# Where the second group's last projections stand, and what the warm-up products read

## The chip, the cores and the metric

The kernel runs on one core of one Trainium2 chip. The metric is the time of one execution on the device in microseconds (us). Engines are named as in the profile: PE does matrix products, PEld loads their weights, DVE, ACT and POOL do elementwise work, SP issues transfers (POOL and ACT issue some too). PE writes its results into PSUM, which DVE and ACT read; everything else lies in SBUF or in device memory.

## What is computed

The input x has 2048 rows of 512 numbers. Two branches are computed from it and mixed row by row.

```python
def A(x, wqkv, wo):                       # attention, 32 heads of 16, window of 256
    q, k, v = split((x @ wqkv))
    scores = einsum("bhqd,bhkd->bhqk", q, k) * 16 ** -0.5
    scores = where((i - j >= 0) & (i - j < 256), scores, -1e9)
    return einsum("bhqk,bhkd->bhqd", softmax(scores), v) @ wo
def B(x, w_gate, w_up, w_down):           # feed-forward, 1792 wide
    return (silu(x @ w_gate) * (x @ w_up)) @ w_down
g = sigmoid((x * gate_w).sum(-1, keepdims=True))
out = g * A(x) + (1 - g) * B(x)
```

## The kernel before

All products are float32 products made of three cheaper ones: each operand is split into a rounded high part and a low rest (`split`, ACT makes the high part, POOL or DVE the rest), and high x high, high x low and low x high are summed in PSUM.

The 2048 rows are cut into four columns `c` of 512, the 32 heads into eight groups `g` of four. `proj(g, c)` makes the queries and keys of one group for one column: twelve products over the whole array into one PSUM tile (L231), then ACT copies that tile out (L274, `ev<-pa` or `ev<-pb`) and splits the copy into `X[g, hf]`, where `hf = c // 2` is the half of the rows. `stack(g, hf)` is a set of twelve transfers on SP's queue, L284 and L285, that lay these parts into the tiles QT and KT from which scores are computed. `X[0, 0]` and `X[1, 1]` lie in the same tiles `xhi`, `xlo` of a pool with one buffer; `X[0, 1]` and `X[1, 0]` (`x01`, `x10`) lie in a pool of their own, `vpool`.

The values V are projected by blocks of 128 rows. The first four blocks are whole-array products. The other twelve go by fours: `vproj2` makes two blocks at once in two lanes, each on 64 of the array's 128 rows (L251, `64*128`), into two tiles named `pb` or two named `pa`. Each name has two buffers in PSUM. When a lane pair is done ACT copies both tiles into `vs` (L442), and after each second block POOL issues a store of `vs` to device memory (`vd<-vs`, L445): eight stores in all. `vs` and V's weights `wvh`, `wvl` lie in `vpool` too.

`stage1(g, b)` computes score products (L301) only for their row maxima, which DVE takes (L303). For group 0 these products stand between V's lane products. `put_max` sends the maxima through device memory into a row of QT (L314 to L319). `stage2(g, b)` computes the scores again (L343, into two buffers named `ps2`), ACT takes their exponentials (L345) into a tile `pt`, and POOL masks them.

The part around the change runs in this order: the projections of both groups for columns 0 and 1 (with V's first blocks between), group 0's columns 2 and 3, V's lane blocks with stage 1 of group 0, then group 1's columns 2 and 3 into `pb`, then `stack(1, 1)` and four loads of V (`load_v`, L330). There `vpool` is closed and `ptp`, the pool of the `pt` tiles, takes its memory. The main loop follows: for each step it runs one product of stage 1 of the next group, one of stage 2 of this group, and three lane pairs of another projection or of the feed-forward's gate and up products (L251), first into two `pa` tiles, then into two `pb` tiles; every fourth step it adds the products of the exponentials with V (L367). All engines execute their own queue in the order in which the code was written (`manual_schedule`).

At the very start nine 128x128 products (L206) run on a tile of ones, so that PE is busy before the first data arrive. The tile is a part of `KT[0][0]`, which POOL fills with ones by a memset at L203, and which is later filled again by `fill_rows` (L424).

Of the kernel before, what the change touches and what calls it, by code (L numbers as in the profile page):

```python
# [8 lines left out]
F32 = mybir.dt.float32  # L9
# [6 lines left out]
P = 128  # L16
# [4 lines left out]
NCH = S // CH  # L21
# [14 lines left out]
def gated_mix(ctx, tc, xT, xn, w1a, w1b, wqk, wv, wo, wgu, wd, gw, outT):  # L36
# [4 lines left out]
    nc = tc.nc  # L41
# [49 lines left out]
    def run(gen, n=None):  # L91

        while n is None or n > 0:
            if next(gen, run) is run:
                break
            n = n and n - 1
# [5 lines left out]
    def slot(name, dtype=F32R):  # L102
        return stk.tile([P, S], dtype, name=name)

    def halves_of(t):
        n = t.shape[-1] // 2
        return [t[:, :n], t[:, n:]]

    QT = [[slot(f"q0{pr}") for pr in range(2)]]
    KT = [[slot(f"k0{pr}") for pr in range(2)]]  # L110
# [4 lines left out]
    def products(key, c):  # L115
        wh, wl = WT[key]
        return [(wt[:, k], xt[c][:, k]) for k in range(NK) for wt, xt in ((wh, xhi), (wh, xlo), (wl, xhi))]

    def swapped(todo):

        return [todo[n] for k in range(0, len(todo), 3) for n in (k, k + 2, k + 1)]
# [71 lines left out]
    pp = ctx.enter_context(tc.tile_pool(name="pp", bufs=2, space=PSUM))  # L193
# [4 lines left out]
    with ExitStack() as A:  # L198
        sm = A.enter_context(tc.tile_pool(name="sm", bufs=2))


        ones = KT[0][0][:, :P].bitcast(F32)
        nc.gpsimd.memset(ones, 1.0)  # L203
        warm = pp.tile([P, CH], F32, name="pa")
        for _ in range(9):
            nc.tensor.matmul(warm[:, :P], ones, ones, start=True, stop=True)  # L206
# [8 lines left out]
        def kept():  # L215
            return sm.tile([P, CH], F32, name="ev", bufs=EV)
# [3 lines left out]
        def x_pair(pool=None, name="x"):  # L220
            return tuple((pool or sm).tile([P, 2 * CH], F32R, name=f"{name}{w}", bufs=1) for w in ("hi", "lo"))

        def split_qk(g, hf, cc, raw):
            hi, lo = (t[:, cc * CH:(cc + 1) * CH] for t in X[g, hf])
            split(hi, lo, raw, *act)

        def whole(pool, name, todo, done):

            ps = pool.tile([P, CH], F32, name=name)
            for n, (w, x) in enumerate(todo):  # L230
                nc.tensor.matmul(ps, w, x, start=n == 0, stop=n == len(todo) - 1)  # L231
                if n < len(todo) - 1:
                    yield
            done(ps)
            yield
# [30 lines left out]
        def proj(g, c, pool, name):  # L266

            hf, cc = divmod(c, 2)
            if cc == 0:
                X[g, hf] = x_pair() if g == hf else x_pair(vpool, f"x{g}{hf}")  # L270

            def done(ps):
                raw = kept()
                nc.scalar.copy(raw, ps)  # L274
                split_qk(g, hf, cc, raw)
            todo = products(("p", g), c)
            return whole(pool, name, swapped(todo) if g == c == 0 else todo, done)

        def stack(g, hf):
            for pr in range(2):  # L280
                q, k = (halves_of(t[g % 2][pr])[hf] for t in (QT, KT))
                hi, lo = (x[32 * pr:] for x in X[g, hf])
                for b, (qx, kx) in enumerate(((hi, hi), (hi, lo), (lo, hi))):
                    nc.sync.dma_start(q[b::4].bitcast(F32), qx[:32].bitcast(F32))  # L284
                    nc.sync.dma_start(k[b::4].bitcast(F32), kx[64:96].bitcast(F32))  # L285
# [24 lines left out]
        def put_max(g, hf):  # L310

            mt = sm.tile([P, 32], F32R, name="mt", bufs=1)
            mtt = sm.tile([P, 32], F32, name="mtt", bufs=1)
            nc.vector.tensor_scalar(mt, MX[g, hf].rearrange("p h b -> p (h b)"), -1.0, None, op0=ALU.mult)  # L314
            nc.vector.transpose(mtt, mt.bitcast(F32))
            md = dram.tile([4, NB // 2, 4, 32], F32, name=f"md{g}{hf}")
            nc.sync.dma_start(md.rearrange("h b p q -> p (h b) q"), mtt)
            for pr in range(2):
                nc.sync.dma_start(halves_of(QT[g % 2][pr])[hf][63::64].bitcast(F32),  # L319
                                  md[2 * pr:2 * pr + 2].rearrange("h b p q -> h (b p q)"))  # L320
# [188 lines left out]
            run(proj(0, c, pp, "pa"))  # L509
        stack(0, 1)  # L510
        stack(1, 0)


        first = chain(*(stage1(0, b) for b in range(NB)))
# [12 lines left out]
                put_max(0, 0)  # L527
        run(first)
        put_max(0, 1)
        for c in range(2, NCH):  # L530
            run(proj(1, c, pp, "pb"))
        stack(1, 1)
        for n in range(4):
            load_v(n)
        vp.close()
# [161 lines left out]
        for t in range(G * NB + 1):  # L697
# [6 lines left out]
            for hd in range(4):  # L704
# [10 lines left out]
                if hd == 1 and part == 0:  # L715
                    if t:
                        ag, c = divmod(d - 1, NCH)
# [393 lines left out]
```

## Time and profile before

| | |
|---|---|
| median of three executions | 801.77 us (801.17 to 802.30) |
| the profiled execution's own time | 801.55 us |
| its span, first to last instruction | 799.9 us |
| granted PE clock, mean over the span | 1.000 |
| PE busy | 794.2 us (99%) |
| DVE busy | 626.2 us (78%) |
| ACT busy | 432.6 us (54%) |
| POOL busy | 342.1 us (43%) |
| PE's share of the chain that ended last | 98% |

All times in the views are counted from the start of the span; 1.65 us of the profiled execution lie outside it. A timeline row reads: start, length, engine, line, operation, tiles written and read, shapes, how many; in brackets how long the engine sat idle before it and what released it. A product's length overlaps that of the next one, so the pace of PE is read from start to start: 0.23 us for a 512-wide product, or for a pair of lane products.

### The profile page before, as it was taken

The numbers are of one execution on the slowest core, as the hardware profiler recorded it, in microseconds if no ns is written. First come the engines' busy times: TensorE is split into PE (matmuls) and PEld (weight loads), VectorE is DVE, ScalarE is ACT, GpSimd is POOL, SyncE is SP. The second block draws the span as 40 slices with busy tenths as digits, with TensorE's granted clock in tenths as the row PEclk, the third lists the DMA queues.
The fourth block names the chain that finished last, engine by engine and source line by source line (L and its number), as shares of the span: only waits on it lengthen the run. The fifth ranks groups of instructions, "written<-read, shape, count | busy, mean of one in ns | idle before, by whom it ended". The sixth has DMA issues, their size and how long they took to land.

```text
span 799.9 us, 21441 instructions
## 1 busy us (share of the span) xinstructions
PE 794.2 (99%) x8247; PEld 698.2 (87%) x8247; DVE 626.2 (78%) x1689; ACT 432.6 (54%) x883; POOL 342.1 (43%) x643
## 2 busy tenths in 40 slices
PE   9999999999999999999999999999999999999998
PEld 8888999889889989899998998888988888888886
DVE  5397787878886887878776888888675478899896
ACT  7422556565565567555666656555643235554642
POOL 6712456565546556544656454546740111000112
PEclk9999999999999999999999999999999999999999
DMA  8574515425242453351533516425537898717435
GB/s 302 168 217 147 142 69 137 131 90 151 68 153 81 114 168 103 112 156 59 145 111 120 152 51 195 144 90 186 190 105 251 285 342 293 288 57 272 93 55 104
DMA packets 62107, 121.88 MB, mean 152 GB/s; under 512 B 10868, under 2 KB 19828, under 8 KB 61748
## 3 DMA queue, kind: packets, MB, share of 16 engines
q1 hardware_dynamic: 54756, 99.01, 40.1%
q0 software_dynamic: 7104, 21.24, 9.0%
q8 instruction: 65, 1.06, 0.6%
q14 instruction: 38, 0.31, 0.1%
q10 hardware_dynamic: 144, 0.26, 0.1%
HBM read 55.97 MB, written 39.34 MB: 119 GB/s over the span
## 4 chain that ended last, share of the span: by engine, by line
PE 98%; DVE 2%; issue 0%; POOL 0%; POOLq 0%
PE pa L251 24%; PE pb L251 24%; PE ps L301 7%; PE ps L343 5%; PE ps L367 5%; PE ps L87 4%; PE ps L86 4%; PE ps L85 4%; PE pb L367 4%; PE pa L231 2%; PE pb L231 2%; PE pa L87 2%; PE pb L86 2%; PE pa L86 2%; PE pb L87 2%; PE pb L85 2%
## 5 line engine op out<-in xcount | busy, mean ns | idle before, releaser
L303 DVE CUSTOM_DVE_ANT_0 ps<-ps,mask 128x384 f32<-128x384 f32 (+2 forms) x512 | 268.5, 540 | 99.4 <-PE ps L343 52.1
L345 ACT ACTIVATE pt<-ps 128x384 f32<-128x384 f32 (+2 forms) x512 | 238.0, 474 | 127.5 <-PE ps L343 68.0
L347 POOL TENSOR_SCALAR_AFFINE_SELECT pt<-pt 128x256 f32<-128x256 f32 x256 | 110.7, 433 | 197.4 <-ACT pt L345 195.5
L343 PE MATMUL ps<-q,k 64*128 64x384 f32 (+2 forms) x512 | 162.3, 335 | 0.0
L301 PE MATMUL ps<-k,q 63*128 63x384 f32 (+2 forms) x512 | 159.6, 332 | 0.5 <-DVE mx L303 0.5
L251 PE MATMUL pb<-xhi,wh 64*128 64x512 f32 x512 | 117.0, 396 | 0.0
L251 PE MATMUL pb<-xlo,wh 64*128 64x512 f32 x512 | 115.7, 391 | 0.0
L251 PE MATMUL pa<-xhi,wh 64*128 64x512 f32 x512 | 115.7, 394 | 0.0
L251 PE MATMUL pb<-xhi,wl 64*128 64x512 f32 x512 | 115.6, 391 | 0.0
L251 PE MATMUL pa<-xlo,wh 64*128 64x512 f32 x512 | 114.4, 392 | 0.0
L251 PE MATMUL pa<-xhi,wl 64*128 64x512 f32 x512 | 114.3, 391 | 0.0
L301 PEld LDWEIGHTS ps<-k,q 63*128 63x128 f32 x512 | 88.9, 185 | 13.4 <-DVE mx L303 3.3
L350 POOL TENSOR_SCALAR_AFFINE_SELECT pt<-pt 128x256 f32<-128x256 f32 x224 | 98.4, 439 | 0.0
L343 PEld LDWEIGHTS ps<-q,k 64*128 64x128 f32 x512 | 91.3, 185 | 5.2 <-issue 0.2
L303 DVE DVE_READ_ACCUMULATOR2_ANT mx<- 128x1 f32 x512 | 71.4, 139 | 0.0
L367 PE MATMUL ps<-pt,vg 64*32 64x320 f32 (+4 forms) x1408 | 70.6, 344 | 0.0
L367 PE MATMUL pb<-pt,vg 64*32 64x256 f32 (+3 forms) x1360 | 69.9, 349 | 0.0
L251 PEld LDWEIGHTS pb<-xhi,wh 64*128 64x128 f32 x512 | 63.1, 186 | 4.1 <-DVE o L384 0.3
L251 PEld LDWEIGHTS pb<-xhi,wl 64*128 64x128 f32 x512 | 62.6, 185 | 3.6
L251 PEld LDWEIGHTS pa<-xhi,wl 64*128 64x128 f32 x512 | 61.3, 185 | 3.9
L251 PEld LDWEIGHTS pb<-xlo,wh 64*128 64x128 f32 x512 | 62.6, 186 | 0.2
L251 PEld LDWEIGHTS pa<-xhi,wh 64*128 64x128 f32 x512 | 60.8, 186 | 1.9
(303 smaller groups left out, 1601.0 us busy)
## 6 DMA issues: line engine op xcount, KB each, us to landing
kept_h<-ev SPq DMA_DIRECT2D x52, 256.0 KB
od<-o POOLq DMA_DIRECT2D x32, 256.0 KB, 3.5
raw<-wgu SPq DMA_DIRECT2D x28, 256.0 KB
q<-xhi SPq DMA_DIRECT2D x56, 128.0 KB
k<-xhi SPq DMA_DIRECT2D x56, 128.0 KB
outT<-sg POOLq DMA_DIRECT2D x28, 256.0 KB, 4.0
vd<-vs POOLq DMA_DIRECT2D x8, 672.0 KB, 4.9
vg<-vd SPq DMA_DIRECT2D x32, 168.0 KB
```

The costliest lines, as they stand in the source:

```text
L85: nc.tensor.matmul(ps, lh, rh, start=start and i == 0, stop=False, skip_group_check=skip)
L86: nc.tensor.matmul(ps, lh, rl, start=False, stop=False, skip_group_check=skip)
L87: nc.tensor.matmul(ps, ll, rh, start=False, stop=stop and i == n - 1, skip_group_check=skip)
L231: nc.tensor.matmul(ps, w, x, start=n == 0, stop=n == len(todo) - 1)
L251: mm = nc.tensor.matmul(ps[me], w[r], x[r], start=not second and i == 0, stop=bool(second) and i == n - 1)
L301: nc.tensor.matmul(ps[:, :n], QT[g % 2][pr][r, q0:q0 + P], KT[g % 2][pr][r, k0:k0 + n], start=True, stop=True)
L303: mx = nc.vector.tensor_tensor_reduce(out=ps[:, :n], in0=ps[:, :n], in1=mask[:, 3 * P - n:], scale=1.0, scalar=NEG, op0=ALU.add, op1=ALU.m ...
L343: nc.tensor.matmul(ps[:, :n], KT[g % 2][pr][r, k0:k0 + P], QT[g % 2][pr][r, k0:k0 + n], start=True, stop=True)
L345: BEHIND.append(nc.scalar.activation(pt[:, j, :n], ps[:, :n], AF.Exp, scale=SCALE))
L347: nc.gpsimd.affine_select(out=pt[:, :, :P], in_=pt[:, :, :P], pattern=[[0, 2], [1, P]], compare_op=ALU.is_ge, fill=0.0, base=0, channel_mu ...
L350: nc.gpsimd.affine_select(out=pt[:, :, 2 * P:], in_=pt[:, :, 2 * P:], pattern=[[0, 2], [-1, P]], compare_op=ALU.is_ge, fill=0.0, base=-1, ...
L367: nc.tensor.matmul(AV[g, c][h][32 * j:32 * j + 32, q0 - c * CH:q1 - c * CH], VG[4 * g + kb // 4][o, kb % 4, 17 * j:17 * j + 32], PT[g, kb, ...
```

## The change

Two edits. The warm-up products read an array of ones that the program holds as a constant from its start (one column of 128 numbers, read again and again), in place of the tile that POOL fills; the memset goes. And the 24 products of `proj(1, 2)` and `proj(1, 3)`, with `stack(1, 1)`, move from behind V's lane blocks to ahead of them, behind `stack(1, 0)`.

```diff
-        ones = KT[0][0][:, :P].bitcast(F32)
-        nc.gpsimd.memset(ones, 1.0)
+        ones = nc.const_aps.tensor(1.0, [P, P], F32)
         warm = pp.tile([P, CH], F32, name="pa")
         for _ in range(9):
             nc.tensor.matmul(warm[:, :P], ones, ones, start=True, stop=True)
...
             run(proj(0, c, pp, "pa"))
         stack(0, 1)
         stack(1, 0)
+        for c in range(2, NCH):
+            run(proj(1, c, pp, "pb"))
+        stack(1, 1)
 
 
         first = chain(*(stage1(0, b) for b in range(NB)))
...
         run(first)
         put_max(0, 1)
-        for c in range(2, NCH):
-            run(proj(1, c, pp, "pb"))
-        stack(1, 1)
         for n in range(4):
             load_v(n)
         vp.close()
```

Lines behind the removed memset have a number lower by one in the changed kernel. The order of the instructions shows two places.

ACT, where V's last copies end and the main loop begins. Before (`vs<-pa` are the copies of V's last two blocks, `ev<-pb` and `xhi<-ev` belong to the two projections, `pt<-ps` is the first exponential; names in brackets are the semaphores that an instruction waits for, `DMASW0` to `DMASW7` those of V's eight stores in their order, `DMAHW` those of SP's transfers):

```order
L442 COPY vs_129<-pa 128x8x4x16 [waits DMASW5_49,PE_49,Activation_49]
L442 COPY vs_129<-pa 128x8x4x16 [waits Activation_49]
L274 COPY ev<-pb 128x512 [waits PE_49]
L67 CAST xhi<-ev 128x512 [waits DMAHW3_49,DMAHW2_49,DMAHW4_49,DMAHW1_49,DMAHW6_49,DMAHW0_49,DMAHW7_49,Activation_49,Pool_49]
L274 COPY ev<-pb 128x512 [waits PE_49]
L67 CAST xhi<-ev 128x512 [waits Activation_49]
L345 ACTIVATE pt<-ps_1048 128x384 [waits DMAHW2_49,DMAHW3_49,DMAHW1_49,DMAHW4_49,DMAHW0_49,DMAHW5_49,DMASW7_49,DMAHW6_49,DMASW6_49,DMAHW7_49,PE_49,Pool_49]
```

Now:

```order
L441 COPY vs_128<-pa 128x8x4x16 [waits DMASW5_49,PE_49,Activation_49]
L441 COPY vs_128<-pa 128x8x4x16 [waits Activation_49]
L344 ACTIVATE pt<-ps_1047 128x384 [waits DMAHW2_49,DMAHW1_49,DMAHW3_49,DMAHW0_49,DMAHW4_49,DMASW7_49,DMAHW5_49,DMASW6_49,DMAHW6_49,PE_49,DMAHW7_49,Activation_49,Pool_49]
L67 CAST wh<-raw 128x512 [waits DMAHW1_49]
L344 ACTIVATE pt<-ps_1065 128x384 [waits PE_49]
```

The two copies and casts of the projections stand 13 rows earlier, and the first exponential follows V's last copy directly. In both orders it names the last of V's stores, `DMASW7`.

PE, where whole-array products end and V's lane products begin. Before:

```order
L231 MATMUL pa<-xlo_73,wh 128x512 [waits DVE_49]
L231 MATMUL pa<-xhi_72,wl 128x512
L251 MATMUL pb<-wvh,xhi_68 128x512 [waits PE_49] x2
L251 MATMUL pb<-wvl,xhi_68 128x512 x2
L251 MATMUL pb<-wvh,xlo_69 128x512 x2
```

Now:

```order
L230 MATMUL pb<-xlo_73,wh 128x512
L230 MATMUL pb<-xhi_72,wl 128x512
L250 MATMUL pb<-wvh,xhi_68 128x512 [waits Activation_49] x2
L250 MATMUL pb<-wvl,xhi_68 128x512 x2
L250 MATMUL pb<-wvh,xlo_69 128x512 x2
```

The products ahead of the lanes were group 0's last projection into `pa`; they are now group 1's last projection into `pb`, the name that the lanes write next, and the first lane pair names ACT.

## The prediction

> **What bounds the kernel now.** I read the page first (busy shares, then the chain that ended last), and then the timeline engine by engine between 33 and 85 us, where the moved work lies.
>
> ```profile
> PE 794.2 (99%) x8247; PEld 698.2 (87%) x8247; DVE 626.2 (78%) x1689; ACT 432.6 (54%) x883; POOL 342.1 (43%) x643
> PE 98%; DVE 2%; issue 0%; POOL 0%; POOLq 0%
> ```
>
> PE is the bound: 99% busy, and 98% of the chain that ended last. So any time in which PE stands still in the middle is added to the end, and moving PE's work about can win only what PE loses today. The place of the change, on PE's timeline:
>
> ```profile
> 33.15 0.39 PE L231 MATMUL pa<-xhi,wl 128*128 128x512 f32 x1
> 33.47 0.50 PE L251 MATMUL pb<-wvh,xhi 64*128 64x512 f32 x2
> ...
> 71.82 0.39 PE L251 MATMUL pa<-wvh,xlo 64*128 64x512 f32 x2
> 72.05 0.34 PE L301 MATMUL ps<-k,q 63*128 63x384 f32 x2
> 72.31 0.50 PE L231 MATMUL pb<-xhi,wh 128*128 128x512 f32 x1
> ...
> 77.68 0.39 PE L231 MATMUL pb<-xhi,wl 128*128 128x512 f32 x1
> 78.00 0.32 PE L301 MATMUL ps<-k,q 63*128 63x128 f32 x1
> 78.00 0.44 PE L343 MATMUL ps<-q,k 64*128 64x384 f32 x1
> ...
> 79.79 0.44 PE L343 MATMUL ps<-q,k 64*128 64x384 f32 x1
> ```
>
> The reader should see that nothing waits here. V's lanes end at 72.05 with the last two products of stage 1; the 24 projection products run from 72.31 to 77.68; the main loop starts at 78.00, and its third stage 2 product stands at 79.79. The only loss is at switches between whole-array and lane products: 0.26 + 5.37 + 0.32 = 5.95 us from 72.05 to 78.00, where 24 products and the one stage 1 pair ahead of them would take 5.44 + 0.17 = 5.61 at the pace of the whole-array products elsewhere:
>
> ```profile
> 22.66 10.88 PE pa L231 x48
> ```
>
> This row of the chain of waits gives 10.88 / 48 = 0.2267 for one 512-wide product, so 5.44 for 24, and 0.17 for a 384-wide one.
>
> What runs meanwhile on the other engines:
>
> ```profile
> 72.30 1.08 ACT L442 COPY vs<-pa 128x512 f32<-128x512 f32 x2 [2.23 <-issue]
> 78.11 0.59 ACT L274 COPY ev<-pb 128x512 f32<-128x512 f32 x1 [1.44 <-PE pb L231]
> 78.73 0.62 ACT L67 CAST xhi<-ev 128x512 fp32r<-128x512 f32 x1
> 79.25 0.48 ACT L345 ACTIVATE pt<-ps 128x384 f32<-128x384 f32 x1
> ```
>
> ```profile
> DMA to landing us min/median/max: 4.7/4.7/4.7
> ```
>
> ```profile
> 73.67 0.89 POOL L445 DMA_DIRECT2D vd<-vs  x1 [2.42 <-ACT vs L442]
> ```
>
> The landing row is that of this last store alone. V's last copies end at 73.38, POOL issues the store at 73.67, and it lands 4.7 us later, at 78.37. The first exponential writes into memory that the closed `vpool` held, and it names that store among its waits. Today it starts at 79.25 behind ACT's cast, 0.88 us after the landing, so the wait costs nothing. The projections are what hides it: they fill 72.3 to 78.0.
>
> **Edit 1, the warm-up.** It removes one memset from POOL and a wait of PE.
>
> ```profile
> 0.81 0.14 POOL L61 MEMSET edge<- 128x56 f32 x1 [0.29 <-POOLq L1103]
> 0.88 0.20 POOL L203 MEMSET k<- 128x128 f32 x1
> 1.09 0.91 DVE L424 MEMSET q<- 128x1024 f32 x1 [1.09 <-PEq L1103]
> 1.14 4.21 PE L206 MATMUL pa<-k 128*128 128x128 f32 x18 [1.14 <-POOL k L203]
> ```
>
> ```profile
> 4.06 0.62 ACT L67 CAST xhi<-q 128x512 fp32r<-128x512 f32 x1
> 5.00 0.77 PE L231 MATMUL pa<-xhi,wh 128*128 128x512 f32 x1
> ```
>
> PE starts at 1.14, 0.06 after the memset's end (0.88 + 0.20). Without it PE starts as soon as it is released: between 0.81, when POOL does, and 1.09, when DVE starts with an instruction that waits for no data. Behind the warm-up the first real product could go from 5.00 to 4.74 at the earliest, since its cast ends at 4.68. So the gain is 0.05 to 0.26 us. I take 0.15, between the two engines' starts, and none as the lower end, because no product in the trace reads one column again and again; were each of the 18 records a tenth slower, 0.4 us would be lost instead (an estimate). POOL's later memsets no longer wait for PE, which is worth nothing: POOL's next work then waits for ACT.
>
> **Edit 2, ahead of the lanes.** The same 24 products, copies, casts and 12 transfers are issued, so no work is added; only waits change. On PE the last projection starts its last product at 33.15 + 24 x 0.2267 = 38.59. The first lane pair needs both `pb` buffers, and one of them is the projection just finished. Its copy starts 0.43 after the start of the last product (78.11 - 77.68) and takes 0.59: the buffer is free at 39.61 and PE goes on at 39.67, with the 0.06 of the warm-up's wait. Without this it would start at 38.59 + 0.32 = 38.91. **Cost 0.76**, or 0.2 less since the first lane may run one product ahead: I take 0.66. So V's lanes and stage 1 run 5.44 + 0.66 = 6.1 us later than now. On ACT this copy stands behind the cast of the projection before it, which overwrites `xhi` and must wait until `stack(0, 0)` has been read out:
>
> ```profile
> 33.70 0.60 SPq L285 DMA_DIRECT2D k<-xhi  x1
> ```
>
> ```profile
> 37.17 0.22 PE L301 MATMUL ps<-k,q 63*128 63x128 f32 x2
> ```
>
> The last of those transfers is issued at 33.70, and the product at 37.17, which reads what they bring, runs on PE's pace; so they have landed by then, the cast is over by 37.9, and the copy, due at 39.02, is not held. On SP the twelve transfers of `stack(1, 1)` now stand ahead of `put_max(0, 0)`; behind the 57.9 at which `stack(1, 0)` is issued today they take 12 x 0.64 = 7.7 us at the pace of 33.70, to 65.6, and the maxima come at about 63.5 + 6.1 = 69.6: covered, by 4 us. V's loads move forward.
>
> **Edit 2, behind the lanes.** Now the main loop follows the lanes directly. First the PSUM buffers: the loop's first stage 2 product needs a `ps2` buffer that DVE still reads, and its first lane pair needs both `pa` buffers.
>
> ```profile
> 72.42 0.57 DVE L303 CUSTOM_DVE_ANT_0 ps<-ps,mask 128x384 f32<-128x384 f32 x1
> 72.90 0.60 DVE L303 CUSTOM_DVE_ANT_0 ps<-ps,mask 128x384 f32<-128x384 f32 x1
> ```
>
> In times of the run before, to which 6.1 is added, the `ps2` buffers come free at 72.99 and 73.50, the `pa` buffers when ACT's copies end, the second at 73.38. So PE, which could start the loop at 72.22, does its first two steps by about 74.9. The third stage 2 product needs the first `ps2` buffer back, that is the first exponential; and that one waits for the store: it starts at 78.37 + 0.06, takes 0.48, and PE goes on at 78.97. **PE stands still from 74.9 to 78.97, 4.1 us.** Behind the waiting exponential ACT holds the next weight's cast and all further exponentials, and behind these POOL's masks and PE's whole queue.
>
> **The sum.** The third stage 2 product, today at 79.79, comes at 78.97 + 6.1 = 85.07: +5.28. As a check by pieces: +0.66 for `pb`; the loop's first two steps last 78.97 - 72.22 = 6.75 instead of 79.79 - 78.00 = 1.79, +4.96; and what went from 72.05 to 78.00 takes 5.44 ahead of the lanes plus 0.17 instead of 5.95, -0.34: together +5.28. With the warm-up's -0.15: +5.1. PE is the bound from there to the end, so the delay stays. On the profiled execution's own 801.55 (span 799.9 and 1.65 around it) that is 806.7; this execution stands 0.2 below the median of 801.77, so I forecast **806.9**.
>
> **The rivals.** First, *the clock falls in the gap*, and it costs more.
>
> ```profile
> 795.58 0.28 PE L87 MATMUL pa<-hh,xlo 128*128 128x256 f32 x1
> ```
>
> ```profile
> 798.80:799.00 0.20, 0.00 (x0) 0.00 (x0) 0.00 (x0) 0.00 (x0) 0.00 (x0) 1.00 0.00 0
> 799.20:799.40 0.20, 0.00 (x0) 0.00 (x0) 0.00 (x0) 0.00 (x0) 0.00 (x0) 0.50 0.00 0
> ```
>
> ```profile
> 6.43 0.63 PE L231 MATMUL pa<-xhi,wh 128*128 128x512 f32 x1
> 6.86 0.58 PE L231 MATMUL pa<-xlo,wh 128*128 128x512 f32 x1
> ...
> 7.51 0.40 PE L231 MATMUL pa<-xhi,wh 128*128 128x512 f32 x1
> 7.74 0.39 PE L231 MATMUL pa<-xhi,wl 128*128 128x512 f32 x1
> ```
>
> PE's last product ends at 795.86, and some 3.3 us later the granted clock is 0.50. The new gap is longer than that. At the start products stand 0.43 apart, and 0.23 from 7.5 on, after 6 us of work. If the clock falls before PE is back, work runs at half pace for 3.3 us (if the rise takes as long as this fall) to 6.1 (as at the start, 1.14 to 7.27): 1.7 to 3.0 us more, 808.6 to 809.9. Against it: the trace shows a single fall, only 0.8 us shorter than the gap, and nothing says that every gap of this length brings one; chance 0.25. The Trainium skill (TensorE: Matmul & The Clock Gate, part 1) says that activity is judged in free-running windows of about 3.4 us; by that rule a gap of 4.1 holds a whole window in about (4.1 - 3.4) / 3.4 = 2 of 10 executions, an estimate. The 3.3 us at the end of this trace agree.
>
> Second, *the first exponential is not really held until the store lands*: the list of names shows a wait, the trace only that it is over. Then the buffers alone cost: +0.66, the loop's first two steps 74.9 - 72.22 = 2.7 instead of 1.79, -0.34 and -0.15 give +1.1, 802.9. Against it: nothing else would be late today either, so the trace cannot refute it. Chance 0.06.
>
> Third, on the other side, *not slower*: PE keeps its pace at the seam because the store and both buffers come free in time, and only the two saved switches and the warm-up count: -0.34 - 0.15, 801.3. Then the third stage 2 product would stand 1.79 behind the loop's start, at 74.01, its exponential would start by 73.47, and the store would have to land with V's last copy, against 5.0 us later today (78.37 - 73.38). Chance 0.04.
>
> Fourth, *the cast into `xhi` waits longer*: if `stack(0, 0)` is read out later than 38.4, every us beyond that delays the copy and the lanes by a us; 807.9 for one. The row at 37.17 speaks against it. Chance 0.05.
>
> The forecast itself has 0.60; its bounds are 4.5 to 5.7 us (a landing in 4.4 to 4.9, the least and the median of the eight stores, the lane's 0.2 and the warm-up's 0.05 to 0.26), 806.3 to 807.5.
>
> ```profile
> DMA to landing us min/median/max: 4.4/4.9/6.7
> ```
>
> The most, 6.7, is of stores in the midst of `stack`'s transfers, of which none runs beside the last one. The range takes in most of the clock's case: **805.4 to 809.7**. 0.2% of the time, 1.6 us, is about what a measurement tells from no change; the cases two and three and a little beside lie within it or below: faster 0.02, same 0.08, slower 0.90.
>
> **What would show it.** Right: a row of ACT's first exponential waiting some 4 to 5 us for the transfer `vd<-vs`, PE idle for about 4 us near 81 to 85, a hole of 0.6 to 0.8 at 39 before the first lane pair, stage 1's first product near 42.2, the first record on PE near 1.0. Wrong: an exponential within 1 us of V's last copy, or PE busy through 85. A granted clock of 0.50 after the gap would be the first rival. The forecast fails as a whole if the memory of `pt` does not wait for the store.

## The result and the profile after

The changed kernel takes 809.84 us (median; 809.77 to 810.0) against 801.92 for the kernel before (801.17 to 802.3): a ratio of 1.0103, 95% interval 1.0091 to 1.0115. It is slower, as forecast, but by 8 us and not by 5: the time lies 0.14 us above the range's upper end of 809.7, where rival 1 (808.6 to 809.9, chance 0.25) had put it. The profiled execution took 809.83, with a mean granted clock of 0.996 where the one before had 1.000.

The page of the kernel after, busy shares and the chain that ended last:

```profile
span 808.1 us, 21435 instructions
PE 797.8 (99%) x8247; PEld 703.9 (87%) x8247; DVE 625.9 (77%) x1689; ACT 432.6 (54%) x883; POOL 341.5 (42%) x642
PE 87%; DVE 2%; issue 1%; ACT 0%; ACTq 0%
```

PE is the bound still, with the same number of products. It was busy 3.6 us longer and the span is 8.2 longer, so some of the loss is standing still and some is work that went slower. Both are at one place. First the end of V's lanes on ACT and POOL (timelines of the kernel after; line numbers are lower by one than before):

```profile
78.16 1.08 ACT L441 COPY vs<-pa 128x512 f32<-128x512 f32 x2 [2.22 <-issue]
84.70 0.49 ACT L344 ACTIVATE pt<-ps 128x384 f32<-128x384 f32 x1 [5.47 <-DMA md<-mtt]
```

```profile
79.53 0.89 POOL L444 DMA_DIRECT2D vd<-vs  x1 [2.41 <-ACT vs L441]
```

```profile
DMA to landing us min/median/max: 4.9/4.9/4.9
```

V's last copies end at 79.24, the store is issued at 79.53 and lands at 84.43 (the last row is of this store alone), and the first exponential starts at 84.70. The profile puts its 5.47 us of waiting down to `md<-mtt`, a transfer of the maxima; an experiment below shows that it is the store. PE at the same place:

```profile
80.74 0.22 PE L300 MATMUL ps<-k,q 63*128 63x128 f32 x1
85.25 0.69 PE L342 MATMUL ps<-q,k 64*128 64x384 f32 x1 [4.18 <-ACT pt L344]
...
85.84 0.94 PE L250 MATMUL pa<-xlo,wh 64*128 64x512 f32 x2
86.27 0.94 PE L250 MATMUL pa<-xhi,wl 64*128 64x512 f32 x2
...
91.52 0.56 PE L250 MATMUL pb<-xhi,wh 64*128 64x512 f32 x2
91.75 0.56 PE L250 MATMUL pb<-xlo,wh 64*128 64x512 f32 x2
```

PE stands still for 4.18 us; the row at 85.25 is the main loop's third stage 2 product, which stood at 79.79 before: +5.46. Then pairs of lane products follow each other 0.43 us apart, and from 91.4 on 0.23. The same stretch by windows (columns: window, length, busy time of PE, PEld, DVE, ACT and POOL with their counts, granted PE clock, DMA share, GB/s):

```profile
84.50:84.60 0.10, 0.00 (x0) 0.00 (x0) 0.00 (x0) 0.00 (x0) 0.00 (x0) 0.80 0.00 0
84.57:87.97 3.40, 2.72 (x14) 2.72 (x16) 0.36 (x2) 2.26 (x5) 2.02 (x4) 0.50 0.34 103
87.98:91.38 3.40, 3.40 (x20) 3.40 (x19) 0.98 (x4) 0.98 (x2) 0.96 (x3) 0.50 0.61 180
91.30:91.40 0.10, 0.10 (x4) 0.10 (x2) 0.00 (x0) 0.00 (x0) 0.10 (x1) 0.56 0.00 0
```

The clock falls to 0.50 at 84.56 (0.80 in the first row is 0.06 us at 1.00 and 0.04 at 0.50), 0.69 us ahead of PE's return, and rises at 91.39. The end of the span:

```profile
803.86 0.28 PE L87 MATMUL pa<-hh,xlo 128*128 128x256 f32 x1
```

This last product stood at 795.58: +8.28, which is the whole difference between the two profiled executions (809.83 - 801.55). Of it 5.46 is lost by the third stage 2 product, 2.68 from there to 92.4, each product set against the same one of before, and 0.14 in all the rest.

### The profile page after: what moved, and what is told of

It reads as the page before. It is cut to its first block, busy times and chain, and to the rows that moved or that the text cites. A ratio compares the mean times of both kernels' runs of the same rounds, so it can differ in the third digit from the quotient of the medians.

```text
span 808.1 us, 21435 instructions
## 1 busy us (share of the span) xinstructions
PE 797.8 (99%) x8247; PEld 703.9 (87%) x8247; DVE 625.9 (77%) x1689; ACT 432.6 (54%) x883; POOL 341.5 (42%) x642
## 4 chain that ended last, share of the span: by engine, by line
PE 87%; DVE 2%; issue 1%; ACT 0%; ACTq 0%
PE pa L250 22%; PE pb L250 22%; PE ps L300 6%; PE ps L342 5%; PE ps L366 5%; PE ps L86 4%; PE ps L85 4%; PE ps L87 4%; PE pb L366 4%; PE pb L86 2%; PE pb L85 2%; PE pa L86 2%; PE pa L85 2%; PE pb L87 2%; PE pa L87 2%; PE pa L775 1%
## 5 line engine op out<-in xcount | busy, mean ns | idle before, releaser
L300 PE MATMUL ps<-k,q 63*128 63x384 f32 (+2 forms) x512 | 167.2, 332 | 0.5 <-DVE mx L302 0.5
L250 PE MATMUL pa<-xhi,wh 64*128 64x512 f32 x512 | 117.4, 396 | 0.0
L300 PEld LDWEIGHTS ps<-k,q 63*128 63x128 f32 x512 | 94.9, 186 | 12.5 <-DVE mx L302 3.1
```

The source lines that it names most:

```text
L250: mm = nc.tensor.matmul(ps[me], w[r], x[r], start=not second and i == 0, stop=bool(second) and i == n - 1)
L300: nc.tensor.matmul(ps[:, :n], QT[g % 2][pr][r, q0:q0 + P], KT[g % 2][pr][r, k0:k0 + n], start=True, stop=True)
```

## The experiments

Time of the kernel before beside the first four runs: 801.58 us; beside the next four 801.78; beside the last two 802.03.

### Each edit alone

```diff
-        ones = KT[0][0][:, :P].bitcast(F32)
-        nc.gpsimd.memset(ones, 1.0)
+        ones = nc.const_aps.tensor(1.0, [P, P], F32)
```

> The first edit alone, on the kernel before: the warm-up products read the program's constant, the projections stay behind the lanes. Theory: PE starts 0.29 us earlier (0.85 instead of 1.14), and as PE is the bound this is all that changes: 801.6 us, no hole, granted clock 1.00 up to PE's last product. Rival (what the changed kernel gained at its start came from the clock rising earlier in that execution, not from the edit): 801.9.

801.80 us (801.04 to 802.55), ratio 1.0002 (0.9993 to 1.0011): nothing that can be measured. PE's timeline of this kernel shows why:

```profile
0.85 4.02 PE L205 MATMUL pa<-const-float32-1.0 128*128 128x128 f32 x18 [0.85 <-PEq L1102]
4.68 0.50 PE L230 MATMUL pa<-xhi,wh 128*128 128x512 f32 x1
...
6.87 0.49 PE L230 MATMUL pa<-xhi,wh 128*128 128x512 f32 x1 [0.27 <-ACT wh L67]
```

PE starts 0.29 earlier than before and its first real product 0.32 earlier. But some products later it waits for ACT's casts, and these come when the data come. The third stage 2 product of this execution stands 0.16 later than before: the head start is used up by a wait for data.

```diff
         stack(1, 0)
+        for c in range(2, NCH):
+            run(proj(1, c, pp, "pb"))
+        stack(1, 1)
...
         put_max(0, 1)
-        for c in range(2, NCH):
-            run(proj(1, c, pp, "pb"))
-        stack(1, 1)
```

> The second edit alone: the projections and stack(1,1) ahead of the lanes, the warm-up as before. Theory: the whole loss is here: PE idle for 4.2 us near 81 to 85.5 behind the first exponential, clock 0.50 behind it for some 6.8 us, 810.1 us. Rival (the two edits work together, an earlier start shifts where the idle time falls in the clock's judging, so that without it the clock does not fall): 807.3.

809.02 us (808.02 to 809.3), ratio 1.0089 (1.0075 to 1.0103). Edit 2 alone brings 7.4 us of slowdown, both edits together 7.9. Three of the four executions have a mean clock of 0.995 or 0.996, as all four of the changed kernel have; the one of 808.02 has 0.998, half as long at half clock. The rival without a fall (807.3) was in none. PE's timeline and windows of the profiled execution:

```profile
81.08 0.22 PE L301 MATMUL ps<-k,q 63*128 63x128 f32 x1
85.25 0.69 PE L343 MATMUL ps<-q,k 64*128 64x384 f32 x1 [3.85 <-ACT pt L345]
```

```profile
80.05:83.45 3.40, 1.35 (x14) 0.94 (x10) 0.99 (x7) 0.00 (x0) 0.71 (x1) 1.00 0.67 213
83.47:86.86 3.39, 1.61 (x8) 1.61 (x10) 0.00 (x0) 1.77 (x4) 1.07 (x1) 0.50 0.10 18
86.88:90.28 3.40, 3.40 (x21) 3.40 (x20) 0.85 (x4) 0.98 (x2) 1.67 (x5) 0.50 0.88 263
```

Here the fall comes at 83.46, only 2.2 us after PE's last product, and PE had worked for 1.35 of the 3.40 us before it. So the fall isn't the answer to 3.4 us of standing still. The 810.1 that was expected is 0.8 above the profiled execution and 1.1 above the median. The third stage 2 product stands at 85.25 as in the changed kernel, but the stretch at half clock, 83.46 to 90.29, began 1.1 us sooner, while PE stood still, so 2.2 us are lost behind that product and not 2.7.

### What the exponential waits for

The last two V blocks get tiles of their own in `xhi` and `xlo` and one store each, so that none of the memory that `pt` takes over is still being read by the last store; the seventh store's remains.

```diff
+            if b >= NB - 2:
+                t = LASTV[b % 2]
+                nc.scalar.copy(..., ps.rearrange("p (g j e) -> p g j e", j=4, e=DH))
+                nc.gpsimd.dma_start(vd[:, :, b].rearrange("g p e -> p g e"), t)
+                return
             t = vs[b // 2 % 2]
```

> The changed kernel, but the last two blocks of V are copied into the tiles xhi and xlo (idle there) and stored from them by two transfers of 336 KB, so that the memory which the exponentials take over holds only what the seventh store and those before it read. Theory (the first exponential waits for the landing of the last store out of that memory): it starts behind the seventh store's landing, some 3.7 us earlier, at about 81; PE's hole shrinks to about 0.5 us, the clock stays at 1.00, total 803.3. Rival (the profile names the small transfer md<-mtt as what the exponential waited for; it still lands near 84.6): the exponential at 84.7, 809.8.

803.44 us (803.03 to 804.67), ratio 1.0022 (1.0013 to 1.0031). On ACT and on PE of this kernel:

```profile
81.16 0.49 ACT L344 ACTIVATE pt<-ps 128x384 f32<-128x384 f32 x1 [1.59 <-DMA vd<-vs]
```

```profile
81.70 0.44 PE L342 MATMUL ps<-q,k 64*128 64x384 f32 x1 [0.31 <-ACT pt L344]
```

The exponential no longer stands behind the last store but behind the one before it, 3.5 us earlier, the clock stays at 1.00, and 6.4 us are back. The transfers of the maxima were left as they were; SP issues them here at these times:

```profile
80.51 0.57 SPq L316 DMA_DIRECT2D md<-mtt  x1
85.90 0.98 SPq L318 DMA_DIRECT2D q<-md  x2
```

The exponential starts 0.08 us after `md<-mtt` has been issued, and 4.7 us before the transfers that read what it brings are. So the releaser that the profile named was not the cause.

### The hole before the first lane pair

To this kernel the exchange of the two names was added, so that the first lane pair writes `pa`, which was free.

```diff
-            (a0, a1), (b0, b1) = vproj2(b, pp, "pb"), vproj2(b + 2, pp, "pa")
+            (a0, a1), (b0, b1) = vproj2(b, pp, "pa"), vproj2(b + 2, pp, "pb")
```

> The kernel with the last two V blocks stored from other tiles, and besides the two lane names of V exchanged, so that the first lane pair writes pa, which group 0's projections left long ago, and the last one pb. Theory: the hole of 0.74 us at 39 goes, everything behind it comes that much earlier, the seventh store too: 803.44 - 0.74 = 802.7, with the third stage 2 product near 81.0. Rival (the first lane pair waits for something else, or the seam behind the lanes takes up what was won): 803.2 to 803.6.

802.91 us (802.57 to 803.73), ratio 1.0015 (1.0006 to 1.0024). At the place of the hole, in the changed kernel and then in this one:

```profile
38.62 0.50 PE L250 MATMUL pb<-wvh,xhi 64*128 64x512 f32 x1
39.36 0.49 PE L250 MATMUL pb<-wvh,xhi 64*128 64x512 f32 x1 [0.25 <-ACT ev L273]
```

```profile
38.22 0.39 PE L230 MATMUL pb<-xhi,wl 128*128 128x512 f32 x1
38.54 0.50 PE L250 MATMUL pa<-wvh,xhi 64*128 64x512 f32 x2
```

In the changed kernel the second lane starts 0.74 after the first; here both start together, 0.32 behind the last whole-array product. The third stage 2 product comes at 80.59, 1.11 earlier than without the exchange, of which 0.4 us were there at 33 us already. That leaves 0.7 for the hole, as expected. The medians differ by 0.53 only. Most of what stays above the kernel before, 0.80 of 1.1 us, stands there already at 80.59, where the exponential waits for the seventh store. None of the kernels measured here beats the one before. The two switches that a better order would save are worth 0.34 us by the prediction's estimate, and the interval of these measurements is some 0.7 us to each side.

### Half of the move

```diff
         stack(1, 0)
+        run(proj(1, 2, pp, "pb"))
...
         put_max(0, 1)
-        run(proj(1, 2, pp, "pb"))
         run(proj(1, 3, pp, "pb"))
         stack(1, 1)
```

> Only proj(1, 2) runs ahead of V's lanes; proj(1, 3) and stack(1, 1) stay behind them. Theory (the stall is the last store's landing less the work that stands in front of the main loop): the lanes come 2.72 us (12 products) + 0.66 later, the store lands at 73.38 + 3.4 + 0.3 + 4.9 = 82.0, the first exponential starts at 82.2, the third stage 2 product at 82.75, some 2.9 later than before: 804.4 to 804.6, PE idle for about 1.9 us ahead of it and no fall of the clock, as no window of 3.4 us is mostly idle. Rival (the stall is there whenever the loop's first exponential follows on a store at all, whatever lies between): 4 us of idle again, 807 to 810.

806.02 us (805.65 to 806.85), ratio 1.0057 (1.0043 to 1.0071): 1.5 us more than the theory. PE's timeline and windows:

```profile
80.66 0.22 PE L300 MATMUL ps<-k,q 63*128 63x128 f32 x1
82.56 0.44 PE L342 MATMUL ps<-q,k 64*128 64x384 f32 x1 [1.67 <-ACT pt L344]
```

```profile
80.27:83.66 3.39, 1.72 (x17) 1.36 (x15) 0.56 (x4) 1.65 (x4) 1.84 (x2) 1.00 0.22 64
83.68:87.08 3.40, 3.40 (x21) 3.30 (x20) 0.99 (x5) 1.08 (x3) 2.13 (x5) 0.50 0.68 168
```

The stall went as expected: 12 products left in place shorten it from 4.18 to 1.67 us, and the third stage 2 product is at 82.56 where 82.75 was expected. The clock did not: it fell after a standstill of 1.67 us, in a window in which PE was busy for 1.72 of 3.39 us, and stayed down for one window. All four executions have a mean clock of 0.997 or 0.998. The expectation that so short a hole brings no fall was wrong.

### Products that nobody reads, in the hole

The changed kernel with n products into `pb` tiles ahead of the third stage 2 product (the first kernel: 16 into one tile; the others: half of n into each of two):

```diff
+                if t == 0 and hd == 2:
+                    for _ in range(2):
+                        idle = pp.tile([P, CH], F32, name="pb")
+                        for _ in range(n // 2):
+                            nc.tensor.matmul(idle, xhi[0][:, 0, :P], xhi[0][:, 1], start=True, stop=True)
                 if t < g7:
                     run(s2, 1)
```

> The changed kernel with 16 products added whose result nobody reads, 512 columns each, on PE just ahead of the third stage 2 product, so 3.6 us of work in the 4.2 us in which PE stood idle. Theory (8.3 us = 5.5 from the hole and the wait for pb, 2.8 from half pace behind it): idle at most 0.6 us at a time, granted clock 1.00 throughout, the third stage 2 product still at 85.2, total 807.0. Rival (the time behind the hole is lost to a backlog of ACT, POOL and transfers, the clock only goes along): 809.8 or more.

> The changed kernel with 12 full products in the hole, six into each of two pb tiles: PE is idle for 4.2 - 12 x 0.25 = 1.2 us. Theory 1 (the clock falls after a window of the fixed grid of 3.41 us in which PE works for less than some 45%): the worst window is still some 60% busy, no fall in any execution, 806.9 to 807.9. Theory 2 (any hole of more than about 1 us at this place brings the fall, as the one of 1.67 us did in every execution): 808.5 or more.

> The changed kernel with 8 products that nothing reads, four into each of two pb tiles, at the place where PE stands still (two tiles so that the later use of the two pb buffers stays as it was). PE is then idle for 4.2 - 8 x 0.25 = 2.2 us. Theory 1 (the clock falls after a window of 3.41 us that is wholly idle): no fall in any execution, 806.9 to 807.1. Theory 2 (a window that is mostly idle is enough; in the run of edit 2 alone the window that ended with the fall had 1.25 of 3.41 us busy, and the window that ended 69% busy in the run with 16 products brought none): idle of 2.2 us in a window leaves 36 to 40% of it busy, so the clock falls in some executions, half of them at the most, and these take 808.5 to 809.8.

> As before with 4 such products, two into each tile: PE is idle for 4.2 - 4 x 0.25 = 3.2 us, still less than a window of 3.41. Theory 1 (wholly idle window): no fall in any execution, 806.9 to 807.1. Theory 2 (a mostly idle window is enough, limit near 40% busy): it falls in two thirds or more of the executions, median 808.5 to 809.8.

| products | PE idle after them, us | time, us | executions with a fall |
|---|---|---|---|
| 16 | 0 | 807.91 (807.37 to 808.05) | 0 of 4 |
| 12 | 1.12 | 807.59 (807.47 to 807.84) | 0 of 5 |
| 8 | 1.87 | 808.95 (807.27 to 809.77) | 3 of 5 |
| 4 | 2.93 | 808.55 (807.61 to 809.9) | 2 of 4 |
| none (the changed kernel) | 4.18 | 809.84 (809.77 to 810.0) | 4 of 4 |

A fall is counted where the mean clock is 0.998 or less; the others have 0.999 or 1.0. With 16 products PE has more to do and the kernel is 1.9 us faster: the rows of that kernel show the third stage 2 product at the same place, but at full pace.

```profile
81.21 3.92 PE L708 MATMUL pb<-xhi 128*128 128x512 f32 x16
85.17 0.44 PE L342 MATMUL ps<-q,k 64*128 64x384 f32 x1
```

Windows of the kernels with 4, 8 and 12 products, each on the grid of that execution's clock steps; the clock fell at the end of the first two, and not at the end of the third:

```profile
80.63:84.02 3.39, 1.45 (x8) 0.67 (x4) 0.36 (x2) 0.00 (x0) 0.00 (x0) 1.00 0.67 210
```

```profile
82.11:85.50 3.39, 1.52 (x10) 0.97 (x10) 0.00 (x0) 0.91 (x3) 0.00 (x0) 1.00 0.40 122
```

```profile
82.68:86.08 3.40, 2.28 (x15) 1.69 (x16) 0.00 (x0) 1.71 (x4) 0.63 (x1) 1.00 0.13 33
```

Holes of 1.87 and 2.93 us, shorter than a window, brought a fall in some executions and not in others, so a wholly idle window isn't needed. That is the theory of mostly idle windows. (The 1.25 us that the expectation for 8 products names for the window of edit 2 alone is 1.35 in its row.) Its shares were rough: with 8 products half of the executions at the most were expected to fall, and 3 of 5 did; with 4 two thirds or more, and 2 of 4 did, so that the median of 808.55 stands for neither the two that fell (809.23 and 809.9) nor the two that didn't (807.61 and 807.88).

The kernels with 12 and 16 products come out 0.9 to 1.0 us above what their third stage 2 product gives (84.91 is +5.12, 806.7; 85.17 is +5.38, 806.9). Product against product, the excess arises at two places, 0.7 at 345 us in both, and another 0.3 at 510 with 16. The kernels with 8 and 4 products lose 0.4 to 0.5 at the first of these places too, and the kernels without added products nothing. At 345 a weight's load lands 1.3 to 2 us later with 16 and 12 products, counted from the cast before it; why it does is open.

### What counts as work for the clock

The same with 16 products over 32 of the array's 128 rows:

```diff
-                            nc.tensor.matmul(idle, xhi[0][:, 0, :P], xhi[0][:, 1], start=True, stop=True)
+                            nc.tensor.matmul(idle, xhi[0][:32, 0, :P], xhi[0][:32, 1], start=True, stop=True)
```

> The changed kernel with 16 products that nothing reads in the hole, eight into each of two pb tiles, each of them over 32 of the array's 128 rows instead of all. In time they fill the hole as the 16 full ones did. Theory 1 (what counts for the clock is the time in which PE is busy): no fall in any execution, as with the full ones, 806.9 to 807.9, third stage 2 product near 85.2 and 0.23 from product to product behind it. Theory 2 (what counts is the part of the array at work): a quarter of the rows for 3.9 us is less than half of any window, the clock falls in all or nearly all executions, 808.9 to 810.

810.73 us (809.45 to 811.95), ratio 1.0109 (1.0095 to 1.0123); mean clock 0.995 to 0.998, a fall in 4 of 4. The time is above the 808.9 to 810 expected: in the profiled execution the third stage 2 product comes 1.4 us later than in the changed kernel, and 1.1 of these were there at 20 us already.

```profile
82.09 4.66 PE L709 MATMUL pb<-xhi 32*128 32x512 f32 x16
86.68 0.69 PE L342 MATMUL ps<-q,k 64*128 64x384 f32 x1
```

```profile
81.64:85.03 3.39, 3.39 (x19) 2.55 (x16) 0.53 (x4) 0.00 (x0) 0.00 (x0) 1.00 0.68 213
85.05:88.44 3.39, 3.39 (x13) 2.54 (x13) 0.00 (x0) 1.88 (x4) 1.66 (x3) 0.50 0.20 53
```

PE is busy for the whole window, and the clock falls at its end. So what counts is not the time in which PE is busy: a quarter of the rows was counted as little work.

## Why the prediction was wrong, step by step

Direction and place were right, and the stall came out only 0.3 us larger than said; the failed step is the clock, which the sum put at nothing and rival 1 at a chance of 0.25.

| step | forecast | measured |
|---|---|---|
| warm-up | -0.15 | 0 at the end (alone: ratio 1.0002); in the profiled execution -0.29 up to 33 us |
| hole before the first lane pair | 0.76, 0.66 taken | 0.74; the last `pa` lane 5.87 later (6.1 - 0.15 forecast) |
| PE stands still | 4.1 us, from 81.0 to 85.07 | 4.18, to 85.25 |
| third stage 2 product | +5.13 | +5.46 |
| clock | 0 (chance of a fall 0.25) | +2.68 |
| the rest | 0 | +0.14 |

**Edit 2, ahead of the lanes**: right, and shown by the kernel with exchanged names. **Behind the lanes**: right, and shown by the kernel whose last blocks have tiles of their own. Two sizes were off by 0.2 each: the last store landed after 4.9 us, not 4.7, and the exponential started 0.27 after that, not 0.06. The chain of waits shows what lies in these 0.27 us: short pieces of ACT's queue on the exponential's line.

```profile
84.47 0.04 ACTq L344
84.51 0.04 issue
...
84.66 0.05 issue
84.70 0.50 ACT pt L344
```

The exponential names a dozen semaphores, and ACT seems to go through what is left of them after the last has come. The forecast took the pace of PE with a single wait for that. With these two +5.13 is +5.5, as measured; this alone would have been 807.1 to 807.2, inside the forecast's own range. **Edit 1** won nothing, which was its lower bound. What the step missed is that PE's own later products wait for data.

**The failed step** is the sentence that "nothing says that every gap of this length brings one", with its 0.25: on the strength of it the sum had no term for the clock, and it cost 2.68 us. The Trainium skill (TensorE: Matmul & The Clock Gate, part 1), as the prediction cited it, gives windows of some 3.4 us that run freely. The grid agrees with the traces: in the changed kernel the clock steps lie at 84.56 and 91.39, 6.83 = 2 x 3.41 apart, in the halved move at 83.67 and 87.09, one window apart, and the place of the grid in the program differs from run to run. The Trainium skill speaks there of an idle window for the fall, and the prediction took that as wholly idle, which made its 2 in 10. The changed kernel's own profiled execution cannot decide this, since its grid had such a window:

```profile
81.15:84.55 3.40, 0.00 (x0) 0.00 (x0) 0.35 (x2) 0.00 (x0) 0.00 (x0) 1.00 0.62 193
```

The windows of the other kernels say otherwise: the clock fell after windows in which PE was busy for 1.35, 1.45, 1.52 and 1.72 of 3.4 us, and stayed after one of 2.28. On this reading a hole of 4.18 us leaves no luck: wherever the grid cuts it, one window has at least half of it, 2.09 of 3.41 us, and is at most 39% busy. It fell in all 8 executions of the changed kernel and of edit 2 alone (there the hole is 3.85 us).

The fall alone would not have left the range: 801.55 + 5.13 + 2.68 is 809.4, or 809.6 on the median. The 0.33 us by which the stall was too short in the forecast and the 0.14 of the rest took the time past 809.7.

The trace of before held a hint. At the start the products at 6.43 and 6.86 are 0.43 apart and those at 7.51 and 7.74 0.23; the fall at the end, at 799.13, less 232 windows puts the rise at 7.24. The two windows of this grid ahead of it are these:

```profile
0.42:3.82 3.40, 2.68 (x12) 2.68 (x13) 1.82 (x2) 1.28 (x2) 2.91 (x9) 1.00 0.40 141
3.84:7.23 3.39, 3.39 (x13) 2.96 (x12) 2.24 (x5) 2.68 (x6) 2.47 (x5) 1.00 0.99 315
```

PE worked for 2.68 us of the first, 79%, and the clock did not rise at its end. A window is thus not judged by whether there was any work in it. (The clock's column has no record yet at this place; the pace of the products shows the state.)

Rival 1's price, 1.7 to 3.0, held: 2.68. It came out near its upper end because PE returned 0.69 us into a window, which was then busy for 2.72 of 3.40 and did not raise the clock, so two windows were cold. Where PE returned ahead of the step that ended in the fall (the halved move), one window was, and the price 1.5.

Rivals 2, 3 and 4 are refuted by the 5.47 us of the exponential and the standstill of PE; nothing waited longer for the cast into `xhi`, which started at 36.67, 0.07 behind the end of its copy. Of the signs that were to show it the hole at 39, the standstill at 81 to 85, the first record near 1.0 (0.85), the clock of 0.50 that was to show rival 1, and the exponential's wait came true; stage 1's first product came at 41.74, not 42.2; that it would be put down to `vd<-vs` did not.

## What to carry to other kernels

Work that seems to sit idle in the order, between the last store out of some memory and the first write into it, may be what hides that store: before it is moved, add up what the next instruction on each engine would then wait for. Price a standstill of PE at its length plus a fall of the clock as soon as it is longer than about half a window of 3.4 us (here 1.4 to 2.7 us more; in every execution at 4 us, in some or all of them from 1.7 to 3). A releaser named in the profile can be one of several; what an instruction waits for is shown by taking that thing away.

## What the hardware showed that was not expected

The clock is judged by windows of 3.41 us on a grid that the program doesn't set: its first rise lies between 4.17 and 7.24 us in the twelve profiled executions. At full clock a window in which PE was busy for 51% or less ended in a fall. One with 67% did not, and nor did one with 59% at the end of the kernel with the exchanged names, where the fall came a window later:

```profile
794.89:798.29 3.40, 2.02 (x17) 1.81 (x16) 2.84 (x6) 0.00 (x0) 0.00 (x0) 1.00 0.30 114
```

At half clock a window with 80% brought no rise, and full ones did. Products over a quarter of the rows, busy 100% of the time, ended in a fall as well. So the shares above, of the time in which PE is busy, are only a stand-in for what counts. Between 51 and 59% nothing was measured, and whether rows alone or also columns count was not tried.

In two of the filled kernels a small DVE operation took 1.23 and 1.21 us in place of 0.18, while POOL was at work on an elementwise operation with two operands. First the kernel before, then the one with 16 products, DVE and POOL:

```profile
342.31 0.18 DVE L314 TENSOR_SCALAR mt<-mx 128x32 fp32r<-128x32 f32 x1
```

```profile
347.71 1.23 DVE L313 TENSOR_SCALAR mt<-mx 128x32 fp32r<-128x32 f32 x1
```

```profile
347.61 1.28 POOL L70 TENSOR_TENSOR wl<-raw,wh 128x512 fp32r<-128x512 f32 x1 [2.07 <-PE ps L342]
```

DVE's operation ended at 348.94, 0.05 after POOL's. Where POOL's operation ran at another time it took 0.18. The Trainium skill (SBUF — State Buffer, SBUF: two separate sides) says that DVE and POOL share a pair of ports, and that a POOL operation, or a DVE operation of a kind that takes the pair, holds it for the whole instruction while the other is blocked. These rows agree with it; no run tested it.
